# Parameter columns inside the first FFN1 pass, and cosine's input ahead of GpSimd's phases

## The chip, the cores and the metric

The kernel runs on one core of one Trainium2 chip. The metric is the device time of one execution in microseconds, as the median over several runs. A profiled execution of the same kernel gives the timeline from which everything below is read.

## The reference

The input is x with 2048 rows of 448 values (bf16). Two branches are mixed by a gate for each row.

- Gate: `g = sigmoid(sum(x * gate_w))`.
- Branch a is a diagonal complex state space model with 448 states. With `dt = exp(log_dt)`, `Lam_bar = exp(dt * Lambda)` and `B_bar = ((Lam_bar - 1) / Lambda) * B`, it runs `h = Lam_bar * h + x_t B_bar` over the rows and gives `y = 2 Re(h C) + x * Dskip`.
- Branch b is a feed-forward layer: `silu(x @ w1) @ w2`, with 1792 hidden values.
- The result is `g * a + (1 - g) * b`.

## The kernel before

**Rows.** The 2048 rows are treated as 1024 pairs. An even and an odd row share a partition, so x enters as `XT`, transposed, with four chunks of up to 128 features for even rows (`XT[:, 0:4]`) and four for odd rows, each in two halves of 512 pairs. The FFN is done in four passes c = 0..3: even rows half 0, even rows half 1, odd rows half 0, odd rows half 1. The scan runs over 1024 pairs.

**Order of the work.** Each engine executes its own queue in the order in which the Python program emits operations. A small class `Tracker` records for each named buffer who wrote and who read it last, and adds the semaphore waits. So the place of a call in the program is the place in its engine's queue, and an operation that waits holds everything behind it on that engine. SP's queue carries most DMAs, ScalarE's queue a few.

**The first stage.** x for even rows, half 0, comes in as plain rows (`XH`, in `XN`) and is transposed on TensorE: `turn_x(j)` does four 128x128 transposes of feature chunk j into a PSUM bank (banks 5, 6 and, for j = 2 and 3 together, 7), and `turned_x(j)` copies the bank to `XT[:, j]` on VectorE (L421). The last chunk has only 64 features; a second copy of it is put into partitions 64 to 127 of `XR` (L432, key `XR0a`), so that two 64-row matmuls can be done side by side.

`ffn1_first` (L354) is a generator. It does the first seven blocks of 128 hidden values of pass 0, in PSUM banks 0 to 6, with the feature chunk j as the outer loop: 7 matmuls for j = 0, then 7 each for j = 1, 2 and 3 (L362). It yields after each j, and the program puts other TensorE work in between. Bank 7 is used in turn by warm-up matmuls, by the transposes of chunks 2 and 3, and by the parameter columns.

**Parameters.** `log_dt`, the real and imaginary part of Lambda, and Dskip are loaded as four rows `R`. `rd` (L390) copies the last 64 values into a fourth full group, `mm_cols` (L396) turns the rows into columns with four tiny matmuls in bank 7, and a VectorE copy (L436) brings them to `PV`. From there a chain of small operations on 128x4 values follows. `pts` (L463) and `ptt` (L466) are VectorE's, `pact` (L469) ScalarE's:

- `dt` (exponential on ScalarE), `ph = dt * Lambda_im`, `ar = dt * Lambda_re`, `mag` (exponential on ScalarE).
- `phf`, `phr`, `fr`: the phase in turns, less its whole part.
- `f2`, `f2r`, `f2` again, `f2s`: the same for two rows. GpSimd's phase tables read these.
- `nfr`, `afr`: minus `fr` and its absolute value, the input of the cosine.
- `sn`, `cs`: sine and cosine on ScalarE.
- `rr`, `lr`, `li`, `nli`, `lis`: products for the scan.

`double(i)` (L442) copies the last 64-row chunk of W1 to partitions 64 to 127, `double(0)` for the first seven blocks of hidden values, `double(1)` for the others. After `mag`, ScalarE's queue issues a DMA for a part of W1 (`W1Ee`), and a one-element Silu (L478) brings in the activation table that the later Silus and the sine use.

**GpSimd's phases.** For each of four groups of states, `phases` (L505, L507) multiplies a row of counters by `f2` and rounds it, as two operations on 128x1024 fp32 values on GpSimd. `phases2` (L512) on VectorE subtracts the two. ScalarE then makes sine and cosine tables from that (L517 to L522). Between them VectorE also prepares `BR` and a part of `BT` (L569, L571) and the swapped copy of x for half 1 (`swap_xr`, L237).

**After that.** The Silus of the first seven banks (L372, `ffn1_act`) follow `sn` and `cs` in ScalarE's queue. TensorE goes on with the remaining seven blocks of pass 0 (L332, L345), which reuse the banks as the Silus free them; the first of these, block 7, uses bank 7, and block 8 uses bank 0. Then come the input products `bu` (L734, L746), passes 1 to 3, the second FFN product (`ffn2`, L696, whose pass 0 is read from PSUM by VectorE in L704), and the output products (L909) with the final combination (L930, L933). The scans run on VectorE beside all this.

Of the kernel before, what the change touches and what calls it, by code (L numbers as in the profile page):

```python
# [7 lines left out]
ALU = mybir.AluOpType  # L8
# [138 lines left out]
def gated_mix(nc, A_x, A_Lambda_re, A_Lambda_im, A_B_re, A_B_im, A_C_re, A_C_im, A_log_dt,  # L147
              A_Dskip, B_x, B_w1, B_w2, gate_w, out):
    with ExitStack() as ctx:
        E = ctx.enter_context  # L150
        T = Tracker(nc, ctx)

        def sb(name, shape, dtype):
            return E(nc.sbuf_tensor(name, list(shape), dtype))
# [12 lines left out]
        XR = sb("XR", [128, NK], BF16)  # L167
# [122 lines left out]
        for dst, src, key in ((GWB, gate_w, "GW"), (DB, A_Dskip, "DB")):  # L290
# [11 lines left out]
             writes=["IOTA"])  # L302
# [10 lines left out]
        def nxt():  # L313
            n_bank[0] += 1
            return BANKS[(n_bank[0] - 1) % len(BANKS)]
# [38 lines left out]
        def ffn1_first():  # L354

            banks = [nxt() for _ in range(NFA)]
            for j in range(4):
                for fb, bank in enumerate(banks):
                    up = j == 3 and fb % 2 == 1
                    p = slice(64, 128) if up else slice(0, 128 if j < 3 else 64)  # L360
                    x = XR[p, 0:512] if up else XT[p, j, 0:512]
                    T.op("pe", lambda pe, fb=fb, bank=bank, j=j, p=p, x=x: pe.matmul(  # L362
                        ps[:, bank, :], W1E[p, j, fb * 128:(fb + 1) * 128], x, start=(j == 0), stop=(j == 3)),
                        reads=[f"W1Ej{j}" if j < 3 else "W1Ez0" if up else "W1Ea0", "XR0a" if up else f"XTe0{j}"],
                        writes=[f"ps{bank}"])
                if j < 3:
                    yield
            yield list(enumerate(banks))

        def ffn1_act(c, fb, bank, n=1):  # L370
# [4 lines left out]
        def ffn1(c, f0=0, before_last=None):  # L375
            for f in range(f0, NFB, 4):
                got = ffn1_mm(c, list(range(f, min(f + 4, NFB))))
                if before_last and f + 8 == NFB + 2:
                    before_last()
                while got:  # L380
                    fb, bank = got.pop(0)
                    n = 1
                    if got and bank % 2 == 0:
                        got.pop(0)
                        n = 2
                    ffn1_act(c, fb, bank, n)
                    yield fb

        def rd():
            T.op("dve", lambda e: e.tensor_copy(R[0:4, D:512], R[0:4, 384:448]), reads=["R0", "R1", "R2", "R3"],  # L390
                 writes=["Rd"])
# [17 lines left out]
        xp = [ps[:, b, c0:c0 + 256].bitcast(BF16) for b, c0 in ((5, 0), (6, 0), (7, 0), (7, 256))]  # L409
# [13 lines left out]
        for j in range(2):  # L423
            turn_x(j)
            turned_x(j)
        first = ffn1_first()
        next(first)
        for f in (turn_x, turned_x):
            for j in (2, 3):
                f(j)  # L430
        next(first)
        T.op("dve", lambda e: e.tensor_copy(XR[64:128, 0:512], xp[3][0:64, :]), reads=["ps7"], writes=["XR0a"])  # L432
        rd()
        T.op("pe", mm_cols, reads=["R0", "R1", "R2", "R3", "Rd", "ID"], writes=["ps7"])
        next(first)
        T.op("dve", lambda e: e.tensor_copy(  # L436
            PV[:, :, :], ps[:, 7, 0:32].rearrange("p (t c) -> p t c", c=8)[:, :, 0:4]),
            reads=["ps7"], writes=["PV"])

        def double(i):  # L440
            f = slice(i * FA, (i + 1) * FA)
            T.op("dve", lambda e: e.tensor_copy(W1E[64:128, 3, f], W1E[0:64, 3, f]), reads=[f"W1Ea{i}"],  # L442
                 writes=[f"W1Ez{i}"])
# [3 lines left out]
        def pc(n):  # L447
            if n not in names:
                names[n] = len(names)
            return names[n]  # L450

        def col(n):
            i = pc(n)
            return P[:, i, :]
# [7 lines left out]
        def pts(o, a, s1, s2, op0, op1, ra):  # L462
            T.op("dve", lambda e: e.tensor_scalar(col(o), a, s1, s2, op0, op1), reads=ra, writes=[o])  # L463

        def ptt(o, a, b, op, ra):
            T.op("dve", lambda e: e.tensor_tensor(col(o), a, b, op), reads=ra, writes=[o])  # L466

        def pact(o, a, f, ra, scale=1.0, bias=0.0):
            T.op("act", lambda e: e.activation(col(o), a, f, bias=bias, scale=scale),  # L469
                 reads=ra, writes=[o])  # L470
# [8 lines left out]
        pts("phf", col("ph"), 1.0 / TWO_PI, None, ALU.mult, ALU.bypass, ["ph"])  # L479
        pts("phr", col("phf"), MAGIC, -MAGIC, ALU.add, ALU.add, ["phf"])  # L480
        ptt("fr", col("phf"), col("phr"), ALU.subtract, ["phf", "phr"])
        pts("f2", col("fr"), 2.0, None, ALU.mult, ALU.bypass, ["fr"])
        pts("f2r", col("f2"), MAGIC, -MAGIC, ALU.add, ALU.add, ["f2"])
        ptt("f2", col("f2"), col("f2r"), ALU.subtract, ["f2", "f2r"])
        T.op("dve", lambda e: e.scalar_tensor_tensor(
            c1("f2s", 3), c1("f2", 3), -1.0, SG[:, 0:1], ALU.mult, ALU.mult),
            reads=["f2"] + SGN, writes=["f2s"])
        pts("nfr", col("fr"), -1.0, None, ALU.mult, ALU.bypass, ["fr"])
        ptt("afr", col("fr"), col("nfr"), ALU.max, ["fr", "nfr"])
        pact("sn", col("fr"), AF.Sin, ["fr"], scale=SIN_SCALE)  # L490
        pact("cs", col("afr"), AF.Sin, ["afr", "HP"], scale=-SIN_SCALE, bias=HP[:, 0:1])
        first = next(first)
        ptt("rr", col("mag"), col("mag"), ALU.mult, ["mag"])
        double(1)


        def phase(pt):
# [52 lines left out]
        def skip():  # L550
            for b in range(4):
# [12 lines left out]
             reads=["li"] + SGN, writes=["lis"])  # L564
# [5 lines left out]
             writes=["BTz"] + BTK[2:4])  # L570
# [387 lines left out]
        for fb, bank in first:  # L958
# [8 lines left out]
        f = ffn1(1)  # L967
# [11 lines left out]
              writes=["XR0b", "XR1b"])  # L979
# [69 lines left out]
def bass_gated_mix__ssm_conv_s5__dense_activation_silu__prompt_kernel(nc, *args):  # L1049
    gated_mix(nc, *args)  # L1050
# [28 lines left out]
```

## Time and profile before

| | |
|---|---|
| median of 5 runs | 141.71 us (141.57 to 142.69) |
| the profiled execution | 142.28 us, of which the span of the engines' work is 140.5 us |
| TensorE matmul busy | 134.8 us (96%) |
| VectorE busy | 124.2 us (88%) |
| ScalarE busy | 94.7 us (67%) |
| GpSimd busy | 31.1 us (22%) |
| granted TensorE clock | 1.0 |

All times of the timeline count from the start of the span. In a group's or timeline's row, the part in square brackets is the idle time of that engine just before, and what ended it. A "q" behind an engine's name is its queue of DMA issues or semaphore instructions. A line number can be a helper's: all 128x4 products are L466, and they are told apart by their order.

### The profile page before, as it was taken

How to read it: one execution, taken by the hardware profiler on the slowest of the kernel's cores; microseconds unless marked ns; L12 is line 12 of the kernel's file. 1: busy time of each engine (PE TensorE's matmuls, PEld its weight loads, DVE VectorE, ACT ScalarE, POOL GpSimd, SP SyncE). 2: the span in 40 equal slices, each digit the busy share in tenths (PEclk: the TensorE clock that was granted, in tenths of full speed). 3: DMA queues.
4: the chain of work that ended last, by engine and by line, in shares of the span. 5: the costliest groups of instructions: out<-in, count | busy, mean ns of one | idle time of the engine just before them, and what ended most of it. 6: DMA issues, size and time to landing. Idle time of an engine off the chain costs nothing.

```text
span 140.5 us, 1925 instructions
## 1 busy us (share of the span) xinstructions
PE 134.8 (96%) x715; PEld 64.0 (46%) x723; DVE 124.2 (88%) x151; ACT 94.7 (67%) x157; POOL 31.1 (22%) x36
## 2 busy tenths in 40 slices
PE   7996999999999999999999999999999999999992
PEld 7451343344354543443555443435555555555561
DVE  0259999999999999999999999999999999995463
ACT  0317999989999967995999383977412536879200
POOL 7105899940000000299900000000000000000000
DMA  3999977799762200300300000000000000222124
GB/s 110 350 247 241 110 155 141 184 391 350 147 129 50 58 0 0 73 1 5 75 0 0 0 0 0 5 0 0 0 0 0 5 0 0 98 93 70 41 90 131
DMA packets 24287, 11.77 MB, mean 84 GB/s; under 512 B 16532, under 2 KB 23832, under 8 KB 24280
## 3 DMA queue, kind: packets, MB, share of 16 engines
q1 hardware_dynamic: 22692, 10.57, 30.9%
q10 hardware_dynamic: 1588, 1.11, 2.6%
q8 instruction: 5, 0.08, 0.3%
q14 instruction: 2, 0.02, 0.0%
HBM read 5.51 MB, written 1.84 MB: 52 GB/s over the span
## 4 chain that ended last, share of the span: by engine, by line
PE 92%; DVE 4%; issue 2%; ACT 1%; DVEq 0%
PE ps L696 30%; PE ps L332 22%; PE ps L909 14%; PE ps L734 13%; PE ps L345 4%; PE ps L362 3%; PE ps L746 2%; PE ps L403 2%; DVE P L466 1%; DVE TMPS L933 1%; PE ps L416 1%; DVE P L463 1%; ACT P L469 0%; ACT AT L372 0%; DVE XT L421 0%
## 5 line engine op out<-in xcount | busy, mean ns | idle before, releaser
L696 PE MATMUL ps<-W,AT 128*128 128x448 bf16 x224 | 43.0, 352 | 0.0
L332 PE MATMUL ps<-XT,W1E 128*128 128x512 bf16 x143 | 33.1, 380 | 1.5 <-ACT AT L372 1.2
L696 PEld LDWEIGHTS ps<-W,AT 128*128 128x128 bf16 x224 | 21.8, 98 | 20.9 <-ACT AT L372 0.5
L372 ACT ACTIVATE AT<-ps 128x1024 bf16<-128x1024 f32 (+1 forms) x33 | 27.1, 900 | 4.8 <-PE ps L345 4.5
L332 PEld LDWEIGHTS ps<-XT,W1E 128*128 128x128 bf16 x147 | 13.7, 98 | 20.3 <-issue 3.4
L734 PE MATMUL ps<-XT,BT 128*128 128x512 bf16 x69 | 16.1, 379 | 0.2
L709 ACT ACTIVATE BT<-ps,GT 128x448 bf16<-128x448 f32 x8 | 5.1, 634 | 13.1 <-PE ps L696 13.1
L599 POOL TENSOR_TENSOR P<-P 128x4 f32<-128x4 f32 x5 | 5.6, 1121 | 29.1 <-DVE P L606 28.8
L909 PE MATMUL ps<-CO,VE 128*128 128x448 bf16 (+1 forms) x63 | 11.6, 332 | 0.0
L909 PE MATMUL ps<-CO,HS 128*128 128x448 bf16 x56 | 11.6, 352 | 0.0
L804 DVE TENSOR_TENSOR_SCAN G<-P,Q 128x1024 f32<-128x1024 f32 (+1 forms) x6 | 11.3, 1918 | 0.0
L734 PEld LDWEIGHTS ps<-XT,BT 128*128 128x128 bf16 x72 | 6.8, 98 | 9.0 <-issue 1.3
L756 ACT ACTIVATE VE<-ps 128x1024 bf16<-128x1024 f32 (+1 forms) x8 | 7.3, 918 | 5.1 <-PE ps L746 5.0
L770 DVE SCALAR_TENSOR_TENSOR HS<-VE,P,G 128x512 bf16<-128x512 bf16 (+1 forms) x10 | 8.1, 856 | 0.2
L909 PEld LDWEIGHTS ps<-CO,VE 128*128 128x128 bf16 x63 | 6.1, 98 | 4.7
L909 PEld LDWEIGHTS ps<-CO,HS 128*128 128x128 bf16 x56 | 5.5, 98 | 5.1
L758 ACT ACTIVATE HS<-ps 128x1024 bf16<-128x1024 f32 (+1 forms) x8 | 7.3, 918 | 0.5 <-PE ps L734 0.5
L770 DVE SCALAR_TENSOR_TENSOR G<-VE,P,HS 128x1024 f32<-128x1024 bf16 (+1 forms) x5 | 7.5, 1494 | 0.1
L505 POOL TENSOR_SCALAR FP<-IOTA,P 128x1024 f32<-128x1024 f32 x3 | 5.4, 1807 | 7.9 <-DVE P L466 7.7
L767 DVE TENSOR_TENSOR Q<-G,COS 128x2048 bf16<-128x2048 f32 (+1 forms) x4 | 7.0, 1756 | 0.1
L767 DVE TENSOR_TENSOR Q<-G,SIN 128x2048 bf16<-128x2048 f32 (+1 forms) x4 | 7.0, 1750 | 0.0
L362 PE MATMUL ps<-XT,W1E 128*128 128x512 bf16 (+1 forms) x24 | 6.7, 414 | 0.2 <-DVE XT L421 0.2
(119 smaller groups left out, 200.0 us busy)
## 6 DMA issues: line engine op xcount, KB each, us to landing
W<-in_B_w_dram SPq DMA_DIRECT2D x1, 1568.0 KB, 12.7
XN<-in_A_x_dram SPq DMA_DIRECT2D x1, 896.0 KB, 8.6
out_dram<-OT SPq DMA_DIRECT2D x8, 112.0 KB, 1.7
out_dram<-TMPS SPq DMA_DIRECT2D x7, 112.0 KB, 1.7
W1E<-in_B_w_dram SPq DMA_DIRECT2D x3, 224.0 KB, 4.1
HS<-HS SPq DMA_DIRECT2D x4, 128.0 KB, 2.3
W1E<-in_B_w_dram SPq DMA_DIRECT2D x1, 384.0 KB, 5.5
XN<-in_A_x_dram SPq DMA_DIRECT2D x1, 384.0 KB, 6.8
```

The lines of the kernel that those rows point to most:

```text
L332: ins = pe.matmul(ps[:, bank, :], W1E[:, j, fb * 128:(fb + 1) * 128], XT[:, x0 + j, hs], start=(j == 0 and not rf), stop=(j == 2 and rf))
L345: ins = pe.matmul(ps[:, bank, :], W1E[p, 3, fb * 128:(fb + 1) * 128], x, start=rf, stop=not rf)
L362: T.op("pe", lambda pe, fb=fb, bank=bank, j=j, p=p, x=x: pe.matmul(ps[:, bank, :], W1E[p, j, fb * 128:(fb + 1) * 128], x, start=(j == 0), ...
L372: T.op("act", lambda e: e.activation(a[:, fb:fb + n, :], ps[:, bank:bank + n, :], AF.Silu), reads=[f"ps{bank + i}" for i in range(n)], wri ...
L696: ins = pe.matmul(ps[:, bank, 0:D], a[:, fb, q * 128:(q + 1) * 128], W2[:, fb, :], start=(first and fb == 0), stop=(fb == NFB - 1), skip_g ...
L734: ins = pe.matmul(ps[:, bank, :], bt(slice(0, 128), j, m), XT[:, 4 * odd + j, hs], start=(j == 0 and not rf), stop=(j == 2 and rf))
L756: T.op("act", lambda e: e.activation(VE[:, m0:m0 + n, hs], ps[:, be[0]:be[0] + n, :], AF.Copy), reads=pe_, writes=[f"V{m}_{h}" for m in ms])
L758: T.op("act", lambda e: e.activation(HS[:, m0:m0 + n, 8 + h * 512:8 + (h + 1) * 512], ps[:, bo[0]:bo[0] + n, :], AF.Copy), reads=po_, writ ...
L767: T.op("dve", lambda e: e.tensor_tensor(o, a, b, op), reads=reads, writes=writes)
L770: T.op("dve", lambda e: e.scalar_tensor_tensor(o, a, s, b, ALU.mult, ALU.add), reads=reads, writes=writes)
L804: T.op("dve", lambda e, c=c, init=init: e.tensor_tensor_scan(G[:, c, w], rb, Q1[:, c, w], init, ALU.mult, ALU.add), reads=[f"Q1{c}", "rr", ...
L909: ins = pe.matmul(ps[:, bank, c], state(kt, odd, m), CO[:, m, c], start=False, stop=(m == YB[-1]), skip_group_check=True)
```

## The change

Three things are moved; no arithmetic is added or left out.

1. `ffn1_first` no longer yields after each j. It yields after the last matmul of j = 0, after the second matmul of j = 1, and after the fourth matmul of j = 1.
2. The row copy `rd` and the column matmuls `mm_cols` come ahead of the transposes of x chunks 2 and 3. TensorE's order was: j = 0, transposes 2 and 3, j = 1, columns, j = 2, j = 3. It becomes: j = 0, two matmuls of j = 1, columns, two matmuls of j = 1, transposes 2 and 3, the last three of j = 1, j = 2, j = 3. VectorE's order was: x copies 2 and 3, `XR0a`, `rd`, `PV`, then the chain from `ph`. It becomes: `rd`, `PV`, x copies 2 and 3, `XR0a`, then the chain from `ph`.
3. In the chain, `nfr`, `afr` and `double(1)` come directly after `fr`, ahead of `f2`, `f2r`, `f2` and `f2s`. Before, `nfr` and `afr` came after `f2s`, and `double(1)` after `rr`.

```diff
@@ ffn1_first
                         writes=[f"ps{bank}"])
-                if j < 3:
-                    yield
+                    if (j, fb) in ((0, 6), (1, 1), (1, 3)):
+                        yield
             yield list(enumerate(banks))
@@
         first = ffn1_first()
         next(first)
-        for f in (turn_x, turned_x):
-            for j in (2, 3):
-                f(j)
+        rd()
         next(first)
-        T.op("dve", lambda e: e.tensor_copy(XR[64:128, 0:512], xp[3][0:64, :]), reads=["ps7"], writes=["XR0a"])
-        rd()
         T.op("pe", mm_cols, reads=["R0", "R1", "R2", "R3", "Rd", "ID"], writes=["ps7"])
         next(first)
         T.op("dve", lambda e: e.tensor_copy(
             PV[:, :, :], ps[:, 7, 0:32].rearrange("p (t c) -> p t c", c=8)[:, :, 0:4]),
             reads=["ps7"], writes=["PV"])
+        for f in (turn_x, turned_x):
+            for j in (2, 3):
+                f(j)
+        T.op("dve", lambda e: e.tensor_copy(XR[64:128, 0:512], xp[3][0:64, :]), reads=["ps7"], writes=["XR0a"])
@@
         ptt("fr", col("phf"), col("phr"), ALU.subtract, ["phf", "phr"])
+        pts("nfr", col("fr"), -1.0, None, ALU.mult, ALU.bypass, ["fr"])
+        ptt("afr", col("fr"), col("nfr"), ALU.max, ["fr", "nfr"])
+        double(1)
         pts("f2", col("fr"), 2.0, None, ALU.mult, ALU.bypass, ["fr"])
         pts("f2r", col("f2"), MAGIC, -MAGIC, ALU.add, ALU.add, ["f2"])
         ptt("f2", col("f2"), col("f2r"), ALU.subtract, ["f2", "f2r"])
         T.op("dve", lambda e: e.scalar_tensor_tensor(
             c1("f2s", 3), c1("f2", 3), -1.0, SG[:, 0:1], ALU.mult, ALU.mult),
             reads=["f2"] + SGN, writes=["f2s"])
-        pts("nfr", col("fr"), -1.0, None, ALU.mult, ALU.bypass, ["fr"])
-        ptt("afr", col("fr"), col("nfr"), ALU.max, ["fr", "nfr"])
         pact("sn", col("fr"), AF.Sin, ["fr"], scale=SIN_SCALE)
         pact("cs", col("afr"), AF.Sin, ["afr", "HP"], scale=-SIN_SCALE, bias=HP[:, 0:1])
         first = next(first)
         ptt("rr", col("mag"), col("mag"), ALU.mult, ["mag"])
-        double(1)
```

## The prediction

> **What bounds the kernel now.** I read the page first for shares: TensorE is busy nearly throughout, VectorE is next, and nothing else is near.
>
> ```profile
> PE 134.8 (96%) x715; PEld 64.0 (46%) x723; DVE 124.2 (88%) x151; ACT 94.7 (67%) x157; POOL 31.1 (22%) x36
> ```
>
> So time can only come out of a TensorE hole. The view of waits for the first 20 us (engine and line, what it waited for, us in total, times, longest) has one such hole of size:
>
> ```profile
> ACT P L469 <- DVE P L466: 1.2, 2, 0.9
> ...
> PE ps L332 <- ACT AT L372: 1.2, 1, 1.2
> ```
>
> The chain of waits over 9 to 20 us says how the hole arises (start, us, what):
>
> ```profile
> 10.64 0.18 DVE P L463
> ...
> 11.65 0.17 DVE P L466
> ...
> 12.12 0.97 DVE P L466
> 13.10 0.02 issue
> 13.12 0.30 ACT P L469
> 13.42 0.49 ACT AT L372
> 13.91 0.05 issue
> 13.96 2.12 PE ps L332 x9
> ```
>
> From 9.95 to 13.1 the end is set by VectorE's small parameter operations, then by ScalarE's cosine (L469), then by the first Silu (L372), which frees bank 0 for the ninth FFN block. One small operation takes 0.97 us where its like took 0.17. The timeline over 11.9 to 14.5 shows what stands beside it:
>
> ```profile
> 11.92 1.16 POOL L505 TENSOR_SCALAR FP<-IOTA,P 128x1024 f32<-128x1024 f32 x1 [7.73 <-DVE P L466]
> ...
> 12.12 1.04 DVE L466 TENSOR_TENSOR P<-P 128x4 f32<-128x4 f32 x2
> ...
> 13.16 1.05 POOL L507 TENSOR_SCALAR G<-FP 128x1024 f32<-128x1024 f32 x1
> 13.19 1.27 DVE L442 COPY W1E<-W1E 64x896 bf16<-64x896 bf16 x1
> ...
> 13.96 0.82 PE L332 MATMUL ps<-XT,W1E 128*128 128x512 bf16 x3 [1.15 <-ACT AT L372]
> ```
>
> The held operation is `afr`, cosine's input: it starts 0.2 us after GpSimd's first phase operation and ends with it. The same copy of 64x896 that took 0.39 us at 10.22 takes 1.27 us at 13.19, beside GpSimd's second.
>
> **What the Trainium skill says.** "SBUF — State Buffer", section "Who interferes with whom": VectorE operations with two SBUF inputs, and copies in the two-port modes, share a port pair with GpSimd; the first to start keeps it for the whole instruction and the other fully blocks. The trace agrees: 0.97 us against 0.17, 1.27 against 0.39, and in the other direction GpSimd's phase at 16.73 takes 2.10 us instead of 1.1 beside a 1.2 us VectorE operation. "ScalarE: Activation LUTs", section "What ACT_TABLE_LOAD costs", gives about 1283 ns for a table load; here it is 1.28 us, from 10.66 to 11.94. It is the floor under the sine and cosine that remains.
>
> **The change, part by part.** All sums are against the profiled execution (142.28 us, span 140.5); the median of the runs is 141.71, 0.57 below, so I apply the difference to the median.
>
> *First part, columns ahead of the later transposes.* TensorE's order changes but no instruction is added. After the first seven matmuls (they end their issue at 7.03, unchanged) come two matmuls of 0.216 us, the four column matmuls (0.19 from 9.21 to 9.40 before), two more matmuls, then the eight transposes: these start at 7.03 + 0.43 + 0.19 + 0.43 = 8.08 instead of 7.03. The columns need the four parameter rows. The landing records of the trace give the last at 6.20; VectorE's row copy (0.17) is done by 6.45, before 7.46. The transposes reuse bank 7, so they now wait for the PV copy: it starts 0.27 after the column matmuls, ends near 7.92, and two matmuls cover it with 0.1 to spare. Queued behind it on TensorE is all of FFN1, so any miss is paid in full. W1's second and third blocks landed at 5.85 and 7.26, earlier than either order asks.
>
> On VectorE the three x copies start 0.65 after the first transpose (7.03 to 7.68 before): 8.73, and take 1.2 to the end of the last (7.68 to 8.89): 9.94. Then `ph`. Before, the same copies ended at 8.89, but the row copy, a 0.42 wait for the columns, the PV copy and a 0.27 wait for ScalarE's exponential followed, and `ph` started at 9.95. After, those four are already done and `ph` starts at about 9.96. **The first part moves the start of the parameter chain by nothing**: the x copies take the place of the waits. The third block of W1 waits for its x copy until about 9.29 where TensorE could start at 9.17: 0.12 lost, inside an interval where TensorE later idles anyway. I take 0 for this part, with -0.15 to +0.15 as bounds.
>
> *Second part, `nfr`, `afr`, `double(1)` ahead of `f2`.* GpSimd cannot start before `f2`. `fr` ends at 11.21 as before; `nfr` and `afr` take 0.2 each from start to start and end near 11.61, unhindered. The exponentials and W1Ee's DMA issue on ScalarE's queue (0.40) stay, so the table load still ends at 11.94; the dummy Silu starts at 11.95, the sine 0.11 later, the cosine 0.11 after that, at 12.17 instead of 13.12. The first Silu follows at 12.37 instead of 13.32 (0.20 after the cosine starts, as before), and TensorE's hole ends at 13.96 - 0.95 = 13.01. TensorE reaches it at 12.5 to 12.6. **Gain 0.95 us**, bounded above by the hole itself plus its handoff, 1.2. `double(1)` becomes 0.39 instead of 1.27, off the path: its reader comes at 16.0.
>
> *What is moved behind.* GpSimd starts 0.82 later (`nfr` 0.20, `afr` 0.20, `double(1)` 0.42), at 12.74. Its eight operations of about 1.05 us alternate with VectorE's four of 1.2 us, so the end of that duel moves too, less the turn that `double(1)` no longer takes: the last phase subtraction ends near 26.35, not 25.57. Four readers matter. The first sine table: its phase was ready at 17.84 and I work out 17.4 to 17.5, since two held VectorE operations are gone; ScalarE asks at 19.1. BR: ready about 19.7, asked at 21.1. The swapped x copy (L237) waits for its transpose DMA, landed at 21.04, and for one GpSimd operation: 22.0 instead of 22.38; TensorE asks at 22.7. No DMA is issued by the moved steps, and SP's queue is unchanged. The fourth is the tight one, in the timeline over 49 to 54:
>
> ```profile
> 49.18 2.41 DVE L704 SCALAR_TENSOR_TENSOR IOTA<-ps,GT,XN 128x448 bf16<-128x448 f32 x4
> ...
> 52.90 1.04 PE L746 MATMUL ps<-XT,BT 64*128 64x512 bf16 x8
> ```
>
> VectorE has no idle stretch over 0.11 us from 25.6 to 51.6, so it carries its 0.78 lateness to L704's end: 52.37. The last four of the L746 matmuls overwrite those banks from 53.34; now they ask at 52.39 and, with a handoff of 0.1, start at 52.47. **Cost 0.08**, bounds 0 and 0.4. Farther on VectorE's last scan stage ends at 128.52, later by 0.78, while its next work waits for TensorE until 130.52, earlier by 0.87: 0.35 remain as cover.
>
> Sum: 0 + 0.95 - 0.08 = 0.87, and 0.05 taken off for handoffs: 0.82, so 141.46 for the profiled execution and **140.9** for the median.
>
> **Rivals.** *(a) GpSimd's lateness eats half.* If the duel costs one more GpSimd turn, or the copy L237 slips behind the next one, VectorE is late by 0.78 + 0.4 to 0.6 and L746 gives back 0.4 to 0.6: **141.3**. For it: VectorE has no slack to catch up in. Against: two held operations fewer.
>
> *(b) Slower: the phase duel becomes the bound.* In the old timing, L704 may be late by 53.34 - 51.59 - 0.1 = 1.65 us before TensorE loses anything; beyond that each us is paid in full, and from 2.36 the kernel is over 0.5% slower. If VectorE's in-order subtractions each meet a phase that isn't ready and two GpSimd operations run alone (2 x 1.05), the lateness is 0.78 + 2.1 = 2.88, and the time 141.71 + 1.23 = **142.9**. For it: a delayed start, and subtractions that wait in program order. Against: each phase has a turn in hand by my working.
>
> *(c) It doesn't do what it says.* If ScalarE's first Silu is held by something else (the table load later, the chain start later by the 1.06 that the transposes move), the hole stays: **141.7**.
>
> **How the numbers follow.** Main forecast 0.64, with its own range 140.6 to 141.0; (a) 0.17; (c) 0.04; (b) 0.15. A measurement here can tell about 0.5%, 0.71 us, from no change, so the main forecast, not far beyond, is faster; (a) and (c) are the same; (b) is slower. The range runs from a gain of 1.2 (140.5) to no gain (141.7), and leaves out most of (b).
>
> **What would show it.** Right: PV copied near 7.8, `ph` still near 9.95, `afr` in 0.16 before any GpSimd phase, GpSimd from about 12.75, first Silu near 12.4, the TensorE hole 0.3 to 0.5 instead of 1.15, `double(1)` 0.39. Wrong in the first part: TensorE idle at the transposes, or `ph` off by over 0.2. Wrong in the last: a wait of L746 on L704 over 0.4, or of L332 on L237 near 22.7. The forecast fails if the hole closes and the end doesn't move with it.

## The result, and the profile after

The changed kernel takes 141.3 us (median of 37 runs) against 141.9 us for the kernel before (72 runs beside it): ratio 0.9954, 95% interval 0.9941 to 0.9966, so 0.65 us less (0.48 to 0.84). The ratio is that of the means, 141.33 and 141.99; the medians differ by 0.6. A second group of runs gave 141.36 against 141.91, ratio 0.9963 (0.9946 to 0.9980). It is faster, by a little less than the 0.5% that the prediction took as the least that a measurement here can tell.

The page shows TensorE with the same work in a shorter span:

```profile
span 140.1 us, 1929 instructions
...
PE 135.3 (97%) x716; PEld 63.9 (46%) x723; DVE 121.7 (87%) x151; ACT 94.7 (68%) x157; POOL 32.1 (23%) x36
```

The waits of its first 27 us, in the columns used before:

```profile
DVE FP L512 <- POOL G L507: 3.2, 2, 2.1
...
ACT P L469 <- DVE P L466: 2.1, 1, 2.1
...
PE ps L332 <- ACT AT L372: 0.3, 1, 0.3
```

The hole at L332 is 0.3 us instead of 1.2. New in the list is VectorE waiting for GpSimd's phases (L512 on L507, 3.2 us). ScalarE's 2.1 us at L469 is no loss: its first exponential now runs early and it waits for `ar`. The timeline over 11.6 to 14.6 shows the mechanism:

```profile
11.85 0.16 DVE L466 TENSOR_TENSOR P<-P 128x4 f32<-128x4 f32 x1
...
12.04 0.39 DVE L442 COPY W1E<-W1E 64x896 bf16<-64x896 bf16 x1
...
12.55 0.28 ACT L469 ACTIVATE P<-P,HP 128x4 f32<-128x4 f32 x1
12.74 2.03 ACT L372 ACTIVATE AT<-ps 128x512 bf16<-128x512 f32 x4
...
13.14 1.16 POOL L505 TENSOR_SCALAR FP<-IOTA,P 128x1024 f32<-128x1024 f32 x1 [8.95 <-DVE P L466]
...
13.37 1.47 PE L332 MATMUL ps<-XT,W1E 128*128 128x512 bf16 x6 [0.30 <-ACT AT L372]
```

`afr` (the row at 11.85) takes 0.16 us and `double(1)` 0.39, both done before GpSimd starts at 13.14. The chain of waits confirms what holds the Silu now:

```profile
10.62 0.20 ACT P L469
10.83 0.20 ACTq L222
11.03 0.03 issue
11.06 1.28 ACT L478
12.34 0.01 issue
12.35 0.20 ACT JK L478
12.56 0.28 ACT P L469 x2
12.84 0.49 ACT AT L372
```

From `mag` on it no longer runs through VectorE's small operations but through ScalarE: `mag`, the W1Ee DMA issue, the table load, sine and cosine.

**A trap in comparing these two profiles.** `ph` starts at 10.35, not 9.95, and so everything seems 0.4 us late. Most of that, 0.28 us, isn't the change: the first seven FFN matmuls (L362, TensorE alone) take different times in different executions of one kernel. Here are the kernel before's first profile and its second:

```profile
4.81 2.38 PE L362 MATMUL ps<-XT,W1E 128*128 128x512 bf16 x7 [0.18 <-DVE XT L421]
```

```profile
4.81 1.70 PE L362 MATMUL ps<-XT,W1E 128*128 128x512 bf16 x7 [0.18 <-DVE XT L421]
```

From the first matmul's start to the slot after the seventh (the start of whatever TensorE does next) it is 2.22 us in the one and 1.54 in the other; in the changed kernel's first profile it is 2.50, in its second 1.51. So I read every profile in three legs: from that slot to `ph`, from `ph` to the end of the hole at L332, and from there to the end of the span. In the two kernels that have two profiles, the first two legs agree within 0.02 us; the last one agrees within 0.01 before and within 0.17 in the changed kernel.

| kernel | ratio to before (95%) | median, us | `ph` to hole's end | hole's end to span's end |
|---|---|---|---|---|
| before (two profiles) | | 141.9 | 4.00, 4.00 | 126.58, 126.59 |
| changed (two profiles) | 0.9954 (0.9941 to 0.9966) | 141.3 | 3.03, 3.04 | 126.74, 126.57 |
| columns part alone | 0.9994 (0.9975 to 1.0013) | 141.74 | 4.01 | 126.58 |
| chain part alone | 0.9937 (0.9920 to 0.9954) | 141.0 | 3.03 | 126.75 |
| changed, Dskip product later | 0.9955 (0.9939 to 0.9971) | 141.23 | 3.02 | 126.58 |
| changed, W1Ee issue earlier | 0.9954 (0.9938 to 0.9971) | 141.23 | 2.81 | 126.94 |
| changed, both of these | 0.9942 (0.9924 to 0.9961) | 140.98 | 2.81 | 126.58 |
| changed, one VectorE operation more | 1.0029 (1.0010 to 1.0048) | 142.45 | 3.03 | 127.86 |
| changed, `double(1)` late | 0.9943 (0.9920 to 0.9965) | 140.81 | 3.08 | 126.58 |
| chain part, Dskip later | 0.9928 (0.9901 to 0.9956) | 141.18 | 3.04 | 126.58 |
| chain part, Dskip later, W1Ee before `dt` | 1.0016 (0.9998 to 1.0035) | 142.29 | 2.81 | 127.58 |
| chain part, Dskip later, W1Ee before `mag` | 0.9928 (0.9902 to 0.9954) | 140.85 | 2.81 | 126.59 |

The first leg, from the slot to `ph`, is 2.92 us wherever TensorE has its old order and 3.03 with the new one. In the two kernels with "W1Ee before" in their names no wait is left at L332; there the middle leg ends where the matmul behind the former hole starts.

### The profile page after: what moved, and what is told of

Its sections match the earlier page's. It is cut to its first block, busy times and chain, and to the rows that moved or that the text cites. A ratio compares the mean times of both kernels' runs of the same rounds, so it can differ in the third digit from the quotient of the medians.

```text
span 140.1 us, 1929 instructions
## 1 busy us (share of the span) xinstructions
PE 135.3 (97%) x716; PEld 63.9 (46%) x723; DVE 121.7 (87%) x151; ACT 94.7 (68%) x157; POOL 32.1 (23%) x36
## 4 chain that ended last, share of the span: by engine, by line
PE 92%; DVE 2%; ACT 2%; issue 2%; DVEq 0%; ACTq 0%
PE ps L696 30%; PE ps L332 23%; PE ps L909 14%; PE ps L734 13%; PE ps L345 4%; PE ps L362 3%; PE ps L746 3%; PE ps L403 2%; DVE TMPS L933 1%; ACT L478 1%; PE ps L416 1%; DVE XT L421 1%; ACT AT L372 0%; ACT P L469 0%; DVE XR L438 0%
## 5 line engine op out<-in xcount | busy, mean ns | idle before, releaser
L332 PE MATMUL ps<-XT,W1E 128*128 128x512 bf16 x145 | 33.3, 379 | 0.6 <-issue 0.3
L332 PEld LDWEIGHTS ps<-XT,W1E 128*128 128x128 bf16 x147 | 13.6, 98 | 19.4 <-issue 3.4
L909 PE MATMUL ps<-CO,VE 128*128 128x448 bf16 (+1 forms) x63 | 11.6, 332 | 0.0
L909 PE MATMUL ps<-CO,HS 128*128 128x448 bf16 x56 | 11.6, 352 | 0.0
L362 PE MATMUL ps<-XT,W1E 128*128 128x512 bf16 (+1 forms) x24 | 6.9, 427 | 0.2 <-DVE XT L421 0.2
```

The costliest lines, as they stand in the source:

```text
L332: ins = pe.matmul(ps[:, bank, :], W1E[:, j, fb * 128:(fb + 1) * 128], XT[:, x0 + j, hs], start=(j == 0 and not rf), stop=(j == 2 and rf))
L909: ins = pe.matmul(ps[:, bank, c], state(kt, odd, m), CO[:, m, c], start=False, stop=(m == YB[-1]), skip_group_check=True)
```

## The experiments

**Which part makes the gain.** The first kernel has the new `ffn1_first` and the new order of columns, transposes and copies, but the old chain; the second has only this:

```diff
         ptt("fr", col("phf"), col("phr"), ALU.subtract, ["phf", "phr"])
+        pts("nfr", ...)
+        ptt("afr", ...)
+        double(1)
         pts("f2", ...)
...
-        pts("nfr", ...)
-        ptt("afr", ...)
...
-        double(1)
```

> The columns part alone: TensorE's and VectorE's order of the first pass as in the changed kernel, the chain after fr as in the kernel before. Theory (the gain is all from the order of the chain): the start of ph moves by less than 0.4 us, cosine's input is again held beside GpSimd's first phase (1 us instead of 0.16), the TensorE hole stays at 1.0 us or more, and the time is that of the kernel before within 0.3 us. Rival (early columns are the gain): ph and the first Silu come at least 0.5 us earlier and the time falls by 0.4 us or more.

> The chain part alone: nfr, afr and double(1) ahead of f2, TensorE's order and the x copies as in the kernel before. Theory: first Silu 0.9 us earlier than before (12.4), hole 0.3 to 0.5, time 0.65 to 0.9 us under the kernel before, so as fast as the whole change or a little faster. Rival (both parts are needed): less than half of the whole change's 0.65 us.

The columns alone gave 0.9994, no difference. Their profile (10.2 to 14 us) has the old picture whole, `afr` held beside GpSimd and the hole at 1.28:

```profile
11.20 1.16 POOL L505 TENSOR_SCALAR FP<-IOTA,P 128x1024 f32<-128x1024 f32 x1 [7.00 <-DVE P L466]
...
11.40 1.04 DVE L466 TENSOR_TENSOR P<-P 128x4 f32<-128x4 f32 x2
...
13.23 1.04 PE L332 MATMUL ps<-XT,W1E 128*128 128x512 bf16 x4 [1.28 <-ACT AT L372]
```

The chain alone gave 0.9937, 0.9 us, at least as much as the whole change. That settles it: the chain's order is the whole gain. Whether the 0.11 us by which the columns part delays `ph` shows in the time, the intervals (0.9920 to 0.9954 against 0.9941 to 0.9966) don't settle.

**Whether L704 takes some of it back.** Three kernels, all with the whole change. One moves a Dskip product of 1.09 us behind L704:

```diff
         run(g1, 2)
-        run(g0, 2)
+        run(g0, 1)
```

> The changed kernel with one of the two Dskip products (1.09 us on VectorE) that stand ahead of L704 moved behind it; VectorE's total work is the same. Theory (VectorE's lateness at L704 holds the last four L746 matmuls): L704 ends about 1.1 us earlier, the 0.15 us wait at L746 goes, and the time is 0.75 to 0.85 us under the kernel before instead of 0.65. Rival (that gap is only TensorE's own issue): no change from 0.65 us.

L704 ended 0.9 us earlier in its profile (50.78 against 51.70 in the changed kernel's second), L746 didn't wait, and the time stayed: 0.9955, which is what the rival had forecast. But in that second profile of the changed kernel L746 didn't wait either, though I had expected the wait of the first one again, and the spans are equal, 138.98. TensorE's eight L746 matmuls in the first and the second profile:

```profile
52.32 1.20 PE L746 MATMUL ps<-XT,BT 64*128 64x512 bf16 x8
```

```profile
51.36 1.04 PE L746 MATMUL ps<-XT,BT 64*128 64x512 bf16 x8
```

So by itself this decided nothing: the expected wait of 0.15 is there in some executions (126.74 against 126.57 in the two profiles), and too small for the medians. Where it is there, L704 ends 42.5 us after `ph` (also in the chain part alone), where it isn't, 42.3: VectorE's and GpSimd's operations interleave differently in the two. The next two press on the place from both sides. One reaches L746 earlier, the other makes L704 later:

```diff
         ptt("ar", col("dt"), LRE, ALU.mult, ["dt", "PV"])
+        ld_w3("act", "W1Ee", FB, F_FF)
         pact("mag", col("ar"), AF.Exp, ["ar"])
         double(0)
-        ld_w3("act", "W1Ee", FB, F_FF)
```

> The changed kernel with the W1Ee DMA issue ahead of mag, without moving the Dskip product. In the kernel with both edits the table load came 0.21 us earlier against ph (mag itself takes the rest), and the hole shrank by 0.21. Theory (L704 holds L746): hole smaller by 0.2, wait at L746 larger by 0.2, so the time is that of the changed kernel within 0.1 us. Rival (L704 doesn't hold anything that lasts): 0.2 us under the changed kernel.

The hole's end came 0.22 us earlier, and the rest of the span took 0.37 us longer than without a wait, 0.20 longer than in the changed kernel's first profile. So the wait took back nearly all of it. The time was 141.23 against 141.36 for the changed kernel in the same group: nothing that the intervals can tell. TensorE's timeline over 49.5 to 54 has the eight L746 matmuls, in one row of 1.04 us before, split by a wait:

```profile
51.95 0.61 PE L746 MATMUL ps<-XT,BT 64*128 64x512 bf16 x4
52.75 0.61 PE L746 MATMUL ps<-XT,BT 64*128 64x512 bf16 x4 [0.19 <-DVE IOTA L704]
```

The row names L704 as what ended it. The 0.19 counts only the idle time; from start to start the fifth matmul comes 0.36 us late. The other kernel does one gate product twice, at the same place, ahead of L704:

```diff
+        run(gate(), 1)
         run(g1, 2)
         run(g0, 2)
```

> The changed kernel with one more VectorE operation of 1.08 us ahead of L704 (the first gate product is done twice, to the same place). Theory (VectorE is at its limit at L704, and each further us is paid in full): L704 ends 1.1 us later, the wait at L746 grows to 1.1 to 1.3 us, and the time is 0.9 to 1.1 us over the changed kernel, so slower than the kernel before by 0.2 to 0.5. Rival (TensorE has slack there): less than 0.3 us over the changed kernel.

It took 142.45, by the medians 1.09 us and by the ratios 0.94 us over the changed kernel in that group, and is slower than the kernel before (1.0010 to 1.0048). The same two rows:

```profile
51.15 0.61 PE L746 MATMUL ps<-XT,BT 64*128 64x512 bf16 x4
52.84 0.61 PE L746 MATMUL ps<-XT,BT 64*128 64x512 bf16 x4 [1.08 <-DVE IOTA L704]
```

An operation of 1.08 us costs about 1 us; the span behind the hole is longer by 1.12 us than in the changed kernel's first profile. With the change VectorE has next to no slack left at this place. Before, the fifth L746 matmul started 1.75 us after L704's end, and where it waits it starts 0.06 us after it: 1.7 us to spare. The chain's gain of 0.97 brings L746 nearer, and VectorE's own delay of 0.70 or 0.87 takes the rest.

**What the remaining hole is.** Both edits together, the Dskip product later and the W1Ee issue earlier ("the one before" in the expectation is the kernel with only the Dskip product moved):

> As the one before, and with the issue of the W1Ee DMA on ScalarE's queue moved ahead of mag, where ScalarE waits anyway. Theory (the table load, late by that 0.40 us issue, is the floor under the first Silu, and L704 the next limit): table load, cosine and first Silu 0.40 to 0.43 us earlier than in the changed kernel, the remaining hole of 0.3 us closed, L746 not held, time 1.1 to 1.3 us under the kernel before. Rival (the Silu is held by cosine's input or the blocks, not by the table): 0.65 to 0.85 us under it.

The table load came 0.50 us after `ph` instead of 0.71 or 0.72, and the hole's end 2.81 after it instead of 3.03 or 3.04, so ScalarE's queue is the floor, as thought. But an issue of 0.40 us gave only 0.22, since the issue had run beside `mag` itself (10.62 to 10.83, issue 10.63 to 11.03). The time was 140.98, by the ratio 0.8 us under the kernel before and not the 1.1 to 1.3 that I expected; its interval (0.9924 to 0.9961) overlaps that of the changed kernel. Set against the kernel that has the DMA edit alone, the span behind the hole is 0.36 us shorter: that is L746's wait, gone with the Dskip product moved.

**Which of the moved operations counts.** `double(1)` back behind `rr`:

> The changed kernel with double(1) left where the kernel before had it, after rr; nfr and afr stay ahead of f2. Theory (cosine's input alone makes the gain): first Silu and hole as in the changed kernel, GpSimd 0.4 us earlier, double(1) held beside GpSimd at about 1.2 us, VectorE at L704 no later than in the changed kernel, time within 0.15 us of it. Rival (the 0.9 us that double(1) costs beside GpSimd come back at L704): wait at L746 larger by 0.3 or more and 0.3 to 0.5 us over the changed kernel.

The hole's end is 0.04 to 0.05 us later, the last subtraction of the phases and with it L704 come 0.6 to 0.8 us earlier (L704's end 41.7 after `ph` instead of 42.3 to 42.5), and the time is 140.81 (0.9920 to 0.9965), which the intervals don't tell from the changed kernel. `double(1)` was held, as before, and no cost of that shows:

```profile
11.50 1.16 POOL L505 TENSOR_SCALAR FP<-IOTA,P 128x1024 f32<-128x1024 f32 x1 [7.31 <-DVE P L466]
...
11.70 1.22 DVE L442 COPY W1E<-W1E 64x896 bf16<-64x896 bf16 x1
```

So `nfr` and `afr` make the gain; `double(1)` ahead of `f2` only makes GpSimd start 0.55 us later (2.79 us after `ph` instead of 2.24), and uses up the slack at L704.

**Toward a better kernel.** The chain part with the Dskip product later, and then with the W1Ee issue moved too, at first ahead of `dt`, where ScalarE has 4.5 us of idle time:

> The chain part alone with one Dskip product moved behind L704. Theory: L746 finds L704 done, so 0 to 0.15 us faster than the chain part alone, that is 0.8 to 1.0 us under the kernel before. Rival: a VectorE operation put later is missed at the end, where VectorE's cover was worked out as 0.35 us, and the time rises by up to 0.2.

> The chain part alone, with the Dskip product moved behind L704 and the W1Ee DMA issued ahead of the first exponential (dt). From what was measured: 0.85 to 0.9 us for the chain part, 0.2 for the table load, 0.1 for L746, so 1.1 to 1.2 us under the kernel before. If the earlier W1Ee transfer delays the transposes that follow it, less.

> The chain part alone, one Dskip product moved behind L704, and the W1Ee DMA issued ahead of mag instead of ahead of dt: about 5 us later than in the kernel whose transposes it delayed. Theory (that delay was the whole loss): the transposes for half 1 land as in the changed kernel, near 20.3 to 21.1, no wait of TensorE for them, and the time is 0.9 to 1.1 us under the kernel before. Rival (the chain part and the DMA edit don't add up for another reason): not faster than the chain part alone.

The first gave 0.9928, which the intervals don't tell from the chain part alone. The second was a miss: 142.29 us, though no wait is left at its hole. Its waits over 15 to 30 us say why:

```profile
DVE XR L237 <- DMA XT<-in_A_x_dram: 2.2, 1, 2.2
DVE BT L569 <- DMA BT<-in_A_B_im_dram: 1.9, 1, 1.9
...
PE ps L332 <- DMA XT<-in_A_x_dram: 0.4, 1, 0.4
```

The 288 KB of W1Ee were issued at 3.98 us, just behind SP's first transpose, and overlapped with it and the next. The third kernel differs only in this issue, and its landing records stand beside: the first transpose came at 13.12 instead of 10.16, and SP's later issues followed late. So the last transpose for odd rows, half 0, came at 18.99 instead of 17.90 and the one for even rows, half 1, at 22.67 instead of 20.74. TensorE waited for both:

```profile
19.08 1.46 PE L734 MATMUL ps<-XT,BT 128*128 128x512 bf16 x6 [0.28 <-issue]
...
23.09 2.75 PE L332 MATMUL ps<-XT,W1E 128*128 128x512 bf16 x12 [0.40 <-DMA XT<-in_A_x_dram]
```

From start to start it lost 0.44 us at the first and 0.56 at the second, which is the 1.0 us by which its last leg is longer. The view puts the first down to "issue"; that it is the transpose is read from its landing, 0.09 us before the start. The second waited for the transpose by way of the swapped copy L237, which VectorE did from 22.70 to 22.99. Why one transfer holds the other up isn't shown. With the issue ahead of `mag`, about 5 us later, the third has no such wait on TensorE (126.59) and 140.85 us: 1.0 us under the kernel before (0.65 to 1.4). Its ratio, 0.9928, is the lowest here, together with the first of these three; the intervals tell neither from the chain part alone or from the changed kernel.

## Why the prediction was right, and by how much not

- **The hole's cause and the chain part.** Predicted 0.95 us by way of an unhindered `afr`, cosine and Silu; measured 0.97 (4.00 to 3.03). `afr` took 0.16, `double(1)` 0.39, GpSimd started 0.82 us later against `ph` (2.79 instead of 1.97), as worked out. This was no luck: each step came as it was derived.
- **The columns part.** I took 0 with bounds of 0.15; it delays `ph`, and with it the hole's end, by 0.11. The mis-sized term is the column matmuls' 0.19, which I took from the old place, from the first one's start to the next FFN matmul. In the new place TensorE gives them 0.28 us, from the end of the slot ahead to the next FFN matmul: 0.10 pass before the first one starts, and that was left out. The transposes came 1.15 us after the slot instead of 1.05, and the x copies and `ph` with them. By the letter of the prediction's sign (`ph` off by over 0.2) the first profile, with `ph` at 10.35, would count as wrong; the sign was set in absolute time, which the spread of the first seven matmuls moves. The rest of the step held: PV was copied in time, the transposes didn't wait, and `ph` gained nothing.
- **The duel moved behind.** Predicted lateness of VectorE 0.78 us; against `ph`, the first scan operation came 0.70 or 0.87 us later in the two profiles. The three covered readers were covered.
- **L746.** Predicted cost 0.08 with bounds 0 and 0.4; measured 0 and 0.16 in the two profiles. The place, the price of a further delay and the point from which it is paid in full, all from rival (b), are borne out by the extra operation: with it L704 comes 1.98 us later against `ph` than before, so (b)'s sum gives 1.98 - 1.65 = 0.33, with the columns 0.44, and the measured loss is 0.41 (0.14 to 0.68). What (b) feared, subtractions that find their phase not ready, happened too (the 3.2 us of L512 on L507 in the first profile), yet the delay stayed near 0.8: from GpSimd's start to the first subtraction only two of VectorE's small operations were held for about 1 us, against four before, and that subtraction came 1.6 us earlier against `ph`. Rival (a), half eaten, isn't what happened, though its number was 141.3: of 0.97, the columns take 0.11 and L746 at most 0.16.
- **The sum.** 0.97 - 0.11 - (0 to 0.16) is 0.70 to 0.86; predicted 0.82; measured 0.65 (0.48 to 0.84) and 0.52 (0.28 to 0.76). The direction and the wide range, 140.5 to 141.7, held. The main forecast's own range, 140.6 to 141.0, did not: the medians are 141.3 and 141.36, the number that rival (a) stood for, and the gain is under the 0.5% line that was to part the main forecast from (a). The traces decide for the main forecast's mechanism; the number alone would not. Three things lie between 140.9 and the median: the columns' 0.11, L746's wait in some executions, and a kernel before that came out at 141.9 rather than the 141.71 of the five runs I started from. The 0.05 taken off for handoffs had no reason behind it, and no run shows it; it made up for half of the columns' 0.11 by luck. Why the second group measured less than the terms add up to stays open; its interval reaches to 0.76.

## What to carry to other kernels

Where a chain of tiny VectorE operations feeds both GpSimd and the critical path, emit those for the critical path first: here a 0.16 us operation that came 0.2 us behind the start of a 1.16 us GpSimd instruction cost 1 us. Moving a producer earlier gains nothing while its consumer's queue still has other work in front; look at where the consumer starts, not at where the producer ends. A gain of this kind uses up slack elsewhere: before counting the next one, list what the delayed engine must have finished, and when it is asked for, and before moving a DMA issue into idle time, look at the transfers that it will overtake.

## What the runs showed that I had not expected

- The first seven FFN matmuls take 1.5 to 2.5 us in different executions of one kernel: start to start 0.43 us at first in some, 0.216 throughout in others, though the warm-up matmuls ahead are the same. It moves the whole rest of the kernel by up to 1.0 us, and is larger than the change. The granted clock reads 1.0 in the slow ones as in the quick ones, so it doesn't tell them apart. What decides it stays open.
- In the changed kernel two 128x4 products that started 0.01 and 0.08 us after GpSimd's first phase took 0.15 us each, and only the third, 0.15 us after it, was held to its end and took 1.02 (the row at 13.14 below is the three of them in 1.16 us). Both profiles of the changed kernel show it. So coming second did not by itself mean being held, which the rule that the prediction cites does not cover; what draws the line between 0.08 and 0.15 us isn't shown.

```profile
13.14 1.16 DVE L466 TENSOR_TENSOR P<-P 128x4 f32<-128x4 f32 x3
```

- The Trainium skill's page "ScalarE: Activation LUTs", section "What ACT_TABLE_LOAD costs", adds a drain of about 1380 ns to a switch of tables. In the chain of the changed kernel the next activation starts 0.01 us after the load's 1.28. No such drain is seen here, and the measurement decides.
